# Key sums of an attention layer turned round on TensorE, with GpSimd adds for the token sums and new plan constants

## The chip, the core and the metric

One core of one Trainium2 chip runs the whole program in one launch. The metric is the device time in microseconds. Three runs of the kernel before took 996.18, 996.35 and 997.45 us; their median, 996.35 us, is the time before.

## What is computed

Random-feature attention feeds a two-layer network with a softplus between the layers (8 batches, 8 heads, 576 tokens, 64 per head, 128 features; 4608 tokens in all, widths 512 and 2048):

```python
def phi(x):
    h = np.einsum('bhsd,md->bhsm', x, omega) - np.sum(x * x, axis=-1, keepdims=True) / 2.0
    return np.exp(h - np.max(h, axis=-1, keepdims=True)) / np.sqrt(m)
q_p, k_p = (phi(q_s), phi(k_s))
kv = np.einsum('bhsm,bhsd->bhmd', k_p, v)
z = np.sum(k_p, axis=2)
num = np.einsum('bhsm,bhmd->bhsd', q_p, kv)
den = np.einsum('bhsm,bhm->bhs', q_p, z)[..., None] + 1e-06
x = (num / den)                       # tokens x 512
h = x @ w_in
y = (np.maximum(h, 0.0) + np.log1p(np.exp(-np.abs(h)))) @ w_out
```

The two sums of the keys are what the change touches: `kv` (features by head width, one matrix for each head) and `z` (the sum of the key features over the tokens).

## The kernel before, in words

Four heads of one batch are a "quad" (`Quad`), so each batch has two and the program has sixteen. The tokens of a quad come in five units: units 0 to 3 hold 128 tokens of each of the four heads, unit 4 the last 64. A unit of keys is loaded, projected onto the features (lines 445 and 588), exponentiated into a tile `ph`, and then summed: `plan_keys` collects the units and `plan_sums` plans their products, units 0 to 2 in one go and units 3 and 4 in a second. In `outer` (line 676) the features of 128 tokens are the stationary operand, 128 columns wide, and the values of the same tokens with a column of ones, 65 columns, are streamed. So one product gives `kv` with features on partitions, and `z` as its last column. Every fp32 product that is no transpose stands twice in a trace; one unit of four products is eight rows of line 676. `part` (682) copies the first go out on ScalarE; `z` (686), `z_turn` (690) and `whole` (694) add the second go on VectorE; `out_z` and `in_z` (700, 704) send `z` through memory to spread it over all partitions.

The queries go the same way up to `ph`, are divided by their denominator (`den` 784, `divide` 794), turned in blocks through memory, and multiplied by `kv` in `plan_both` (954), `plan_x` (997) and `plan_late_x` (1048). There the stationary operand is 64 columns wide and the two heads of a pair write the lower and the upper half of the output partitions. The first batch has a way of its own (735, 868, 877, 922).

The network's two layers are products of 512 columns in three parts each (high by high, high by low, low by high; lines 1412 to 1414 and 1441 to 1443, and 1199 and 1256 to 1258 for the last pair of token blocks). They are most of TensorE's work. `ident` and `idle` products (line 1571, "fill") compute nothing that is used; they stand where the planner expected TensorE to wait in the first 228 us.

The order of every engine is fixed while the program is built. Each piece of work is a `do(...)` with a cost, a due time and what it comes after; `in_order` takes the works one by one, by the engine that could start first and among its candidates by due time, and gives out buffers by name (`room`). The due times are a table (`KEYS`, `QUERIES`, `IN`, `OUT`) plus a constant at each `do`. GpSimd and VectorE share a port to memory, so works marked `port` are put in order with each other.

## Time and profile before

| | us |
|---|---|
| median of three runs | 996.35 |
| profiled execution, first to last instruction (span) | 995.2 |
| TensorE busy | 989.6 |
| VectorE busy | 783.6 |
| ScalarE busy | 722.7 |
| GpSimd busy | 206.4 |

The page gives no other time of the profiled execution than its span; the median of the runs is 1.15 us above it. TensorE's rows overlap: a product of 512 columns is shown as 0.39 us long, while the next one starts 0.227 us later. So what a product costs is read from start to start, not from its length. A group's cost below is the time from the start of the last wide product before it to the start of the second wide product after it, less two steps of 0.227 us: the first wide product after a group is often followed late, and that belongs to the group.

### The profile page before, as it was taken

To read this page: it belongs to the slowest core of one execution; us is meant where nothing else is said; L and a number is where in the kernel's file an instruction comes from. 1 tells how busy PE (TensorE), PEld (TensorE's weight loads), DVE (VectorE), ACT (ScalarE), POOL (GpSimd) and SP (SyncE) were. 2 spreads that over 40 slices of the span, in tenths; PEclk is the share of its full clock that TensorE was granted. 3 is DMA by queue.
4 is the path that set the end of the run, shared out by engine and by line. 5 is a ranking of instruction groups with operands and counts; after the bars stand their busy time and mean duration, and the time that the engine had idled before them with its cause. 6 is when DMAs were issued, how large, how long until landed. Compare 5 with 4: busy or idle time off the path is not lost.

```text
span 995.2 us, 17488 instructions
## 1 busy us (share of the span) xinstructions
PE 989.6 (99%) x5495; PEld 830.9 (83%) x5495; DVE 783.6 (79%) x2306; ACT 722.7 (73%) x1794; POOL 206.4 (21%) x235
## 2 busy tenths in 40 slices
PE   9999999999999999999999999999999999999998
PEld 8988888888888888888878888888888878888886
DVE  6899986889898888888879886887787958676620
ACT  7999887879777777877777776776776656666520
POOL 3313232312221122101212121112011214223000
PEclk9999999999999999999999999999999999999999
DMA  9982355454464455543454444434542331000011
GB/s 321 352 282 90 111 162 152 138 160 141 136 183 139 125 138 160 159 128 113 138 144 133 123 129 119 155 106 113 138 141 75 80 92 43 0 1 1 1 43 42
DMA packets 117628, 124.49 MB, mean 125 GB/s; under 512 B 16288, under 2 KB 93728, under 8 KB 117536
## 3 DMA queue, kind: packets, MB, share of 16 engines
q1 hardware_dynamic: 117392, 123.26, 41.4%
q8 instruction: 43, 0.70, 0.3%
q14 instruction: 49, 0.40, 0.1%
q10 hardware_dynamic: 144, 0.13, 0.0%
HBM read 97.37 MB, written 25.98 MB: 124 GB/s over the span
## 4 chain that ended last, share of the span: by engine, by line
PE 98%; DVE 1%; ACT 0%; issue 0%
PE banks L1441 11%; PE banks L1412 11%; PE banks L1442 10%; PE banks L1443 10%; PE banks L1413 10%; PE banks L1414 10%; PE banks L1199 8%; PE banks L676 5%; PE banks L588 5%; PE banks L1256 3%; PE banks L1258 3%; PE banks L1257 3%; PE banks L445 2%; PE banks L997 2%; PE banks L735 1%; PE banks L954 1%
## 5 line engine op out<-in xcount | busy, mean ns | idle before, releaser
L1412 PE MATMUL banks<-xh,wi 128*128 128x512 f32 (+1 forms) x512 | 188.8, 369 | 0.4 <-DVE u L1427 0.4
L1413 PE MATMUL banks<-xl,wi 128*128 128x512 f32 (+1 forms) x512 | 186.1, 363 | 0.0
L1414 PE MATMUL banks<-xh,wi 128*128 128x512 f32 (+1 forms) x512 | 185.9, 363 | 0.0
L1441 PE MATMUL banks<-wo,gh 128*128 128x512 f32 x448 | 178.6, 399 | 0.0
L1442 PE MATMUL banks<-wo,gh 128*128 128x512 f32 x448 | 175.5, 392 | 0.0
L1443 PE MATMUL banks<-wo,gl 128*128 128x512 f32 x448 | 175.0, 391 | 0.0
L1418 ACT ACTIVATE u<-banks 128x512 f32<-128x512 f32 (+1 forms) x128 | 70.1, 548 | 73.4 <-PE banks L1414 60.5
L1412 PEld LDWEIGHTS banks<-xh,wi 128*128 128x128 f32 x512 | 96.4, 188 | 17.2 <-issue 1.2
L1414 PEld LDWEIGHTS banks<-xh,wi 128*128 128x128 f32 x512 | 96.4, 188 | 15.6
L1413 PEld LDWEIGHTS banks<-xl,wi 128*128 128x128 f32 x512 | 96.6, 189 | 13.9
L1441 PEld LDWEIGHTS banks<-wo,gh 128*128 128x128 f32 x448 | 84.2, 188 | 18.5 <-issue 4.3
L1443 PEld LDWEIGHTS banks<-wo,gl 128*128 128x128 f32 x448 | 84.1, 188 | 18.5
L1442 PEld LDWEIGHTS banks<-wo,gh 128*128 128x128 f32 x448 | 84.4, 188 | 13.3
L1427 DVE SCALAR_TENSOR_TENSOR u<-banks,u 128x512 f32<-128x512 f32 (+1 forms) x128 | 78.4, 613 | 15.8 <-ACT u L1424 15.4
L612 ACT ACTIVATE phq<-phq,smq 128x128 f32<-128x128 f32 x216 | 71.8, 395 | 14.7 <-DVE smq L608 14.7
L794 POOL TENSOR_TENSOR phq<-phq,dnq 128x512 f32<-128x512 f32 (+1 forms) x46 | 41.9, 911 | 189.2 <-DVE dnq L790 113.1
L612 ACT ACTIVATE phk<-phk,smk 128x128 f32<-128x128 f32 x216 | 71.9, 397 | 10.7 <-DVE smk L608 10.7
L784 DVE CUSTOM_DVE_ANT_0 restq<-phq,zb 128x128 f32<-128x128 f32 x280 | 72.7, 293 | 4.8 <-ACT phq L612 4.0
L1421 ACT ACTIVATE u<-u 128x512 f32<-128x512 f32 (+1 forms) x128 | 74.4, 581 | 1.8
L1424 ACT ACTIVATE u<-u 128x512 f32<-128x512 f32 (+1 forms) x128 | 74.6, 584 | 1.3
L1431 ACT CAST gh<-u 128x512 fp32r<-128x512 f32 (+1 forms) x97 | 55.8, 576 | 18.0 <-PE banks L1442 17.1
L1435 POOL TENSOR_TENSOR gl<-u,gh 128x512 fp32r<-128x512 f32 (+1 forms) x41 | 45.1, 1101 | 106.4 <-ACT gh L1431 31.5
(224 smaller groups left out, 2097.3 us busy)
## 6 DMA issues: line engine op xcount, KB each, us to landing
xk<-ky SPq DMA_DIRECT2D x48, 384.0 KB
xq<-qy SPq DMA_DIRECT2D x48, 384.0 KB
qdq<-restq SPq DMA_DIRECT2D x56, 256.0 KB
out<-o SPq DMA_DIRECT2D x36, 256.0 KB
vk<-vv SPq DMA_DIRECT2D x70, 130.0 KB
rawi<-wi SPq DMA_DIRECT2D x16, 512.0 KB
rawo<-wo SPq DMA_DIRECT2D x16, 512.0 KB
q<-qdq SPq DMA_DIRECT2D x64, 128.0 KB
```

Of the source, the lines that this page charges most:

```text
L612: nc.scalar.activation(b["ph"][:, c], b["ph"][:, c], AF.Exp, bias=b["sm"][:, 2, c : c + 1])
L784: i = nc.vector.tensor_tensor_reduce(jk[r, c], ph[r, c], q.zb[r, h], 1.0, 1e-6, ALU.mult, ALU.add, dn[r, 0, c : c + 1])
L1199: nc.tensor.matmul(b[key], x, y, start=fresh and not kk and not n, stop=kk == 1 and n == 2, skip_group_check=True)
L1412: nc.tensor.matmul(b["h"], wh, xh[:, cc, t], start=cc == 0, stop=False)
L1413: nc.tensor.matmul(b["h"], wh, xl[:, cc, t], start=False, stop=False)
L1414: nc.tensor.matmul(b["h"], wl, xh[:, cc, t], start=False, stop=cc == NCC - 1)
L1421: nc.scalar.activation(b["u"], b["u"], AF.Exp, scale=-1.0)
L1424: nc.scalar.activation(b["u"], b["u"], AF.Ln, bias=1.0)
L1427: nc.vector.scalar_tensor_tensor(b["u"], b["h"], 0.0, b["u"], ALU.max, ALU.add)
L1441: nc.tensor.matmul(acc[tt], gh, w2[fc][:, 0], start=fc == 0, stop=False)
L1442: nc.tensor.matmul(acc[tt], gh, w2[fc][:, 1], start=False, stop=False)
L1443: nc.tensor.matmul(acc[tt], gl, w2[fc][:, 0], start=False, stop=fc == NFC - 1)
```

## The change

In `plan_sums` the operands change places: 64 columns of values are the stationary operand, the 128 features are streamed, and the two heads of a pair write the two halves of the output partitions. `kv` then stands with the head width on partitions and has to be transposed (`kv_turn`, two transposes a quad) and copied (`kv_turned`). The column of ones is gone. `z` is made in two ways. In the second batch (two quads) TensorE makes it with a 32 column stationary operand of ones, four products a unit, into the same bank. In the six batches after it GpSimd adds the feature tiles of the five units (`plan_z`, four adds with the last one in two halves), and `kv_turn` sums that tile over the partitions with four products of 32 columns. `z_row` copies the result, and `out_z` sends it in one transfer instead of four.

Beside that: query blocks of over 256 columns are loaded in two pieces (before, over 320); tiles are laid out so that nearly all large ones start at 448 modulo 512 bytes, where `xh` and `xl` stood at 192 and others at 0, 64, 128, 256 and 320; weight loads may come right behind the first key load; and nearly every cost and due time of the planner has another number, so that the order of all engines is another.

```diff
-KEYS = ((-130.35, -33.11, -44.26, -126.91, -51.00), (-184.12, -170.41, -56.38, -80.88, -261.61))
+KEYS = ((-681.34, -192.75, -318.79, -174.84, -200.15), (-576.11, -262.69, -529.96, -206.80, -300.25))
...
+        if apart:
+            for x in loads:
+                x.behind = ld
...
+        def add():
+            add_ = nc.gpsimd.tensor_tensor
+            x = b["ph", i]
+            if u == 1:
+                q.z = at.tile([P, 4, M], F32, name=f"z{q.nm}", tag=q.z_slots["z"], bufs=1)
+                b0, i0, _ = q.z_first
+                return add_(q.z, b0["ph", i0], x, ALU.add)
+            if u < 4:
+                return add_(q.z, q.z, x, ALU.add)
+            for j in (1, 0):
+                r, h = slice(j * D, (j + 1) * D), slice(2 * j, 2 * j + 2)
+                a_ = add_(q.z[r, h], q.z[r, h], x[r, :2], ALU.add)
+            return a_
...
-            for c in range(4 if u < 4 else 2):
-                end = k == len(keys) - 1 and c == (3 if u < 4 else 1)
-                cs = slice(c, c + 1) if u < 4 else slice(c, 4, 2)
-                nc.tensor.matmul(kv[:, cs], ph[:, c], v[:, cs], start=not k and not c, stop=end, skip_group_check=True)
+            end = k == len(keys) - 1
+            for p in range(2):
+                for j in range(2):
+                    r, c = (slice(0, P), 2 * j + p) if u < 4 else (slice(j * D, (j + 1) * D), p)
+                    nc.tensor.matmul(
+                        kv[j * D : (j + 1) * D, p], v[r, c], ph[r, c], start=not k and not p, stop=end, skip_group_check=True
+                    )
+            for c in range(4 if na > 2 else 0):
+                nc.tensor.matmul(
+                    kv[32 * c : 32 * (c + 1), 2], (ones if u < 4 else halves[:, c // 2 : c // 2 + 1]).broadcast_to([P, 32]),
+                    ph[:, c if u < 4 else c % 2], start=False, stop=end, skip_group_check=True,
+                )
...
+        def kv_turn():
+            y["turned"] = y["bank"][:, 2 * M if na < 3 else 0 :][:, : 2 * M].rearrange("p (a m) -> p a m", m=P)
+            for p in range(2):
+                nc.tensor.transpose(y["turned"][:, p], q.kvp[:, p], ident)
+            for c in range(0 if na > 2 else 4):
+                nc.tensor.matmul(
+                    y["bank"][32 * c : 32 * (c + 1), :M], ones.broadcast_to([P, 32]), q.z[:, c], start=True, stop=True,
+                    skip_group_check=True,
+                )
...
-            sizes = [w] if w <= 320 else [256, w - 256]
-            kinds = ["q" if w <= 256 else "q1"] if w <= 320 else ["q0", "q1"]
+            sizes = [w] if w <= 256 else [256, w - 256]
+            kinds = ["q"] if w <= 256 else ["q0", "q1"]
```

Where the order of the instructions moves, three places matter.

TensorE at the second go of one quad in the middle of the program (batch 3, first quad): before, units 3 and 4 and what follows (`phk` are key features, `vk` values, `wi`, `xh` and `xl` the first layer's operands).

```order
L676 MATMUL banks<-vk_0_3_3287,phk_0_3_3402 128x65 x4
L676 MATMUL banks<-vk_0_4_3374,phk_0_4_3486 128x2x65 x2
L1412 MATMUL banks<-xh,wi_1119 128x512
L1413 MATMUL banks<-xl,wi_1119 128x512
L1414 MATMUL banks<-xh,wi_1119 128x512
```

And now, in the same place:

```order
L727 MATMUL banks<-phk_0_3_3444,vk_0_3_3290 64x128 x4
L727 MATMUL banks<-phk_0_4_3545,vk_0_4_3411 64x128 x4
L1489 MATMUL banks<-xh,wi_510 128x512
L1490 MATMUL banks<-xl,wi_510 128x512
L1491 MATMUL banks<-xh,wi_510 128x512
L1489 MATMUL banks<-xh,wi_510 128x512
L1490 MATMUL banks<-xl,wi_510 128x512
L1491 MATMUL banks<-xh,wi_510 128x512
L748 MATMUL banks<-ident,kvp_0_3436 128x128 x2
L750 MATMUL banks<-z_0_3276,small 32x128 x4
```

The go has eight products instead of six, and six wide products after it stands a new group, the two transposes and the four sums of `z`; between the two VectorE runs `whole`.

SyncE's queue of loads at the start, before (`wi` and `wo` are weights, `k` keys):

```order
L241 DMA omf_76<-om 128x128
L324 DMA rawi_115<-wi 128x1024
L413 DMA xk_0_1_117<-k 128x2x260
L505 DMA x_first<-k 128x260
L413 DMA xk_0_2_121<-k 128x2x260
```

And now:

```order
L247 DMA omf_76<-om 128x128
L331 DMA rawo_120<-wo 128x1024
L331 DMA rawo_122<-wo 128x1024
L331 DMA rawi_124<-wi 128x1024
L517 DMA x_first<-k 128x260
L421 DMA xk_0_1_145<-k 128x2x260
L421 DMA xk_0_2_147<-k 128x2x260
```

Three weight loads of 512 KB, not one, stand ahead of the second key unit.

TensorE in the same stretch, before, from the first fill to the second quad's second key unit:

```order
L1571 MATMUL banks<-ident 128x512
L445 MATMUL banks<-omf,xk_0_1_117 128x128 x4
L457 MATMUL banks<-small,xk_0_1_117 128x56 x4
L1571 MATMUL banks<-ident 128x512
L445 MATMUL banks<-omf,xk_0_2_121 128x128 x4
...
L1571 MATMUL banks<-ident 128x512 x2
L445 MATMUL banks<-omf,xk_1_0_127 128x128 x4
L457 MATMUL banks<-small,xk_1_0_127 128x56 x4
L1571 MATMUL banks<-ident 128x512 x3
L445 MATMUL banks<-omf,xk_1_1_140 128x128 x4
```

And now:

```order
L1648 MATMUL banks<-ident 128x512 x10
L454 MATMUL banks<-omf,xk_0_1_145 128x128 x4
L466 MATMUL banks<-small,xk_0_1_145 128x56 x4
L1648 MATMUL banks<-ident 128x512
L454 MATMUL banks<-omf,xk_0_2_147 128x128 x4
...
L1648 MATMUL banks<-ident 128x512 x8
L454 MATMUL banks<-omf,xk_1_0_153 128x128 x4
L466 MATMUL banks<-small,xk_1_0_153 128x56 x4
L454 MATMUL banks<-omf,xk_1_1_155 128x128 x4
```

The fills on `ident` are 27 in all now, and were 9; the ten on `idle` ahead of everything are the same.

## Rows read from the trace of the kernel before

**Rows 1.** The page: its head, and busy time of each engine.
```profile
span 995.2 us, 17488 instructions
PE 989.6 (99%) x5495; PEld 830.9 (83%) x5495; DVE 783.6 (79%) x2306; ACT 722.7 (73%) x1794; POOL 206.4 (21%) x235
```
**Rows 2.** The chain that ended last: shares of the span by engine.
```profile
PE 98%; DVE 1%; ACT 0%; issue 0%
```
**Rows 3.** Windows: stretch, length, PE, PEld, DVE, ACT, POOL, clock, DMA share, GB/s.
```profile
6.00:20.00 14.00, 13.94 (x169) 11.95 (x168) 8.99 (x30) 11.39 (x40) 5.62 (x9) 1.00 1.04 356
400.00:500.00 100.00, 100.00 (x511) 84.26 (x510) 86.14 (x270) 77.84 (x196) 17.51 (x22) 1.00 0.47 136
```
**Rows 4.** Timeline, TensorE: first and last of 24 wide products; start, length, instruction.
```profile
420.53 0.39 PE L1441 MATMUL banks<-wo,gh 128*128 128x512 f32 x1
...
425.74 0.39 PE L1414 MATMUL banks<-xh,wi 128*128 128x512 f32 x1
```
**Rows 5.** Timeline, TensorE: first go of a quad's key sums, units 0 to 2.
```profile
196.30 0.39 PE L1414 MATMUL banks<-xh,wi 128*128 128x512 f32 x1
196.53 2.79 PE L676 MATMUL banks<-vk,phk 128*128 128x65 f32 x24
...
199.44 0.39 PE L1442 MATMUL banks<-wo,gh 128*128 128x512 f32 x1
```
**Rows 6.** Timeline, TensorE: second go, units 3 and 4.
```profile
212.76 0.40 PE L1443 MATMUL banks<-wo,gl 128*128 128x512 f32 x1
212.99 1.50 PE L676 MATMUL banks<-vk,phk 128*128 128x65 f32 x12
...
214.56 0.40 PE L1442 MATMUL banks<-wo,gh 128*128 128x512 f32 x1
```
**Rows 7.** Timeline, TensorE: eight narrow products (64 columns stationary) over 128 columns.
```profile
668.90 0.39 PE L1443 MATMUL banks<-wo,gl 128*128 128x512 f32 x1
669.22 1.09 PE L954 MATMUL banks<-q,kvs 128*64 128x128 f32 x16
...
670.58 0.40 PE L1442 MATMUL banks<-wo,gh 128*128 128x512 f32 x1
```
**Rows 8.** The same, over 256 columns.
```profile
383.85 0.39 PE L1414 MATMUL banks<-xh,wi 128*128 128x512 f32 x1
384.17 1.95 PE L954 MATMUL banks<-q,kvs 128*64 128x256 f32 x16
...
386.39 0.40 PE L1442 MATMUL banks<-wo,gh 128*128 128x512 f32 x1
```
**Rows 9.** Timeline, TensorE: four transposes, and what starts after them.
```profile
25.52 0.60 PE L868 MATMUL banks<-ident,xq 128*128 128x128 f32 x4
25.95 1.04 PE L735 MATMUL banks<-xk 128*128 128x256 f32 x4
```
**Rows 10.** Groups by form: fills on `ident`; busy, mean ns, idle before.
```profile
L1571 PE MATMUL banks<-ident 128*128 128x512 f32 x9 | 3.7, 462 | 0.1
```
**Rows 11.** Timeline, TensorE: three fills, and the product behind them.
```profile
13.10 0.96 PE L1571 MATMUL banks<-ident 128*128 128x512 f32 x3
13.99 0.71 PE L445 MATMUL banks<-omf,xk 64*128 64x128 f32 x8
```
**Rows 12.** Timeline, TensorE: a wait early in the first layer, and its releaser.
```profile
60.34 0.39 PE L1412 MATMUL banks<-xh,wi 128*128 128x256 f32 x1 [0.40 <-DVE u L1427]
```
**Rows 13.** Groups by form: late wide products with their moving tile at different places.
```profile
L1199 PE MATMUL banks<-xl,wi 128*128 128x512 f32 x64 | 25.0, 390 | 0.0
L1199 PE MATMUL banks<-b,wi 128*128 128x512 f32 x48 | 12.4, 393 | 0.0
```
**Rows 14.** Groups by form: GpSimd add, full and half; `whole` on VectorE.
```profile
L1435 POOL TENSOR_TENSOR gl<-u,gh 128x512 fp32r<-128x512 f32 x27 | 34.9, 1291 | 66.4 <-ACT gh L1431 17.9 <-DVE gh L1431 10.7 <-PE banks L588 9.7
L582 POOL TENSOR_TENSOR tq<-xq,tq 64x256 fp32r<-64x256 f32 x8 | 5.9, 738 | 20.7 <-ACT tq L578 14.5 <-DVE tq L578 6.0
L694 DVE SCALAR_TENSOR_TENSOR kvs<-banks,kvp 128x256 f32<-128x256 f32 x14 | 5.8, 413 | 0.0
```

More of the change, by code (lines that the diff above doesn't have):

```diff
@@ L254, in favor_softplus_kernel @@
     make_identity(nc, eye)
+    for i in range(4):
+        at.tile([P, 3, 8], F32, name=f"sm{i}", tag=f"sm.{i}", bufs=1)
+    at.tile([P, 16], F32, name="gap1")
     nc.gpsimd.tensor_copy(dense, eye)
@@ L260, in favor_softplus_kernel @@
     halves, ones = small[:, :2], small[:, 2:3]
+    for i in range(4):
+        const.tile([P, 4, 4], F32, name=f"dn{i}", tag=f"dn.{i}", bufs=1)
     xh = const.tile([P, NCC, RING], F32R, name="xh")
@@ L357, in plan_weights @@
         l = do(
-            "SP", dma(0.65, 1.60, 1.7), due + 87.17, load, spare={} if last else {"w": 2},
+            "SP", dma(0.65, 1.28, 1.7), due + 110.47, load, spare={} if last else {"w": 2},
             take=[({"i": "qh", "o": "ql"}[nm] if last else "w", box, "raw")],
         )
+        loads.append(l)
         if last:
@@ L614, in plan_split @@
         ld = do(
-            "SP", read(n * (P + D) * P * 4), due - 89.77, load, behind=prev.get("load"), take=[("x", b, "x")],
+            "SP", read(n * (P + D) * P * 4), due - 417.96, load, behind=prev.get("load"), take=[("x", b, "x")],
         )
@@ L661, in plan_keys, with plan_z @@
                 q.keys, q.key_deps = [], []
+    def plan_z(q, b, i, u, due, es):
+        if q.b < 2:
+            return
+        b["uses", ("phs", i)] = 2
+        if not u:
+            q.z_first, q.z_slots = (b, i, es), {}
+            return
+        def add():
[11 more added lines that the diff above has]
+            return a_
+        give = [(b, ("phs", i))]
+        if u == 1:
+            b0, i0, es0 = q.z_first
+            give.append((b0, ("phs", i0)))
+            after = es + es0
+        else:
+            after = es + [q.z_last]
+        q.z_last = do(
+            "POOL", pool(512) if u < 4 else 2 * pool(256), due - 163.51, add, after=after, give=give,
+            take=[("z", q.z_slots, "z")] if u == 1 else [],
+        )
     def plan_sums(q, keys, due, deps):
@@ L698, in out_z @@
-            for i in range(4):
-                r = slice(i * 32, (i + 1) * 32)
-                nc.sync.dma_start(q.zd[:, r], q.zr[i * 32 : i * 32 + 4])
+            q.zd = dram.tile([4, M], F32, name=f"zd{q.nm}", tag="zd", bufs=2)
+            nc.sync.dma_start(q.zd, q.z[::32, 0] if na < 3 else q.kvp[::32, 2])
         def in_z():
@@ L711, in plan_sums @@
             m = do(
-                "PE", 0.86 if u < 4 else 0.43, due - 235.34, lambda k=k: outer(k), after=[m] if k else [x for x, _ in deps],
-                soon={} if k else dict(deps), take=[] if k else [("at" if q.b > 1 else "more", y, "bank")],
+                "PE", (0.50 if u < 4 else 0.31) + 0.30 * (na - 2) + (0 if k else 0.10), due - 259.72, lambda k=k: outer(k), after=[m] if k else [x for x, _ in deps],
+                soon={} if k else dict(deps), take=[] if k else [("at" if q.b > 1 else "more", y, "at")],
                 give=[(b, ("phs", i)), (b, ("vs", i))], heat=1040,
@@ L933, in plan_early_x @@
         t = do(
-            "PE", 0.45 if tail else 0.46, due - 227.12, turn, after=[d for _, d in rows], heat=1024, behind=prev.get("turn_x"),
+            "PE", 0.45 if tail else 0.46, due - 389.27, turn, after=[d for _, d in rows], heat=1024, behind=prev.get("turn_x"),
             take=[("any", y, "b")], give=[(b, "x") for b, _ in rows],
@@ L1349, in plan_pair @@
-            q2 = do(*dp(2 * P), sdue - 139.44, lambda e, b=b: sums(e, 2, b), after=[q1, f1], port=True)
-            q3 = do(*dp(2 * P), sdue - 44.26, lambda e, b=b: sums(e, 3, b), after=[q2], give=[(b, ("tag", "f2"))], port=True)
-            q4 = do(*dp(2 * P), sdue - 32.45, lambda e, b=b: sums(e, 4, b), after=[q2], port=True)
+            sdue = due - 280.32
+            f1 = do(*dp(TB), sdue + 436.12, lambda e, b=b, j=j, nm=nm: whole(e, b, "f1", j, nm), after=gate + [done_w["i", j]], take=[("two", b, ("tag", "f1"))], port=True, behind=pe.get((5, j - 2)))
@@ new lines, in plan_pair @@
+            f2 = do(*dp(TB), sdue + 524.21, lambda e, b=b, j=j, nm=nm: whole(e, b, "f2", j + H, nm), after=gate + [done_w["i", j + H]], take=[("two", b, ("tag", "f2"))], port=True, behind=f1)
+            q1 = do(*dp(2 * P), sdue + 48.46, lambda e, b=b, nm=nm: sum1(e, b, nm), after=[f2], take=[("two", b, ("tag", "R"))], port=True)
+            q2 = do(*dp(2 * P), sdue + 363.85, lambda e, b=b: sums(e, 2, b), after=[q1, f1], port=True)
+            q3 = do(*dp(2 * P), sdue - 20.48, lambda e, b=b: sums(e, 3, b), after=[q2], give=[(b, ("tag", "f2"))], port=True)
```

327 lines of the change are left out of this document (171 added, 156 removed).

## The prediction, made before the changed kernel ran

> **What bounds the kernel now.** I read the page's head first: TensorE is busy 99% of a span of 995.2 us, the next engine 79% [rows 1]. The chain of waits agrees, with 98% of it on TensorE [rows 2]. The windows tell that this holds from early on: TensorE is busy 13.94 of 14.00 us even between 6 and 20 us, and all of 400 to 500 us, at a granted clock of 1.00, which is the 2.4 GHz level [rows 3]. So nothing that another engine gains is worth anything here, and anything that TensorE gains or loses, at the start or later, moves the end by as much. The sum below therefore counts TensorE's time alone. Of the other engines it asks only whether TensorE comes to wait for them.
>
> The unit is the wide product of 512 columns: 24 of them start 5.21 us apart from first to last, 0.227 us each [rows 4].
>
> **The key sums, twelve quads.** Before, a first go costs 199.44 - 196.30 - 2 x 0.227 = 2.69 us [rows 5] and a second one 1.35 us [rows 6], 4.04 us a quad. The new shapes do not stand in the trace; the nearest are narrow groups, 64 columns stationary, where two products write the two halves of the output partitions. Eight of them cost 1.23 us over 128 columns [rows 7] and 2.09 us over 256 [rows 8]. The difference over 8 x 128 more columns gives 0.1075 us per product over 128 columns, and the rest, 0.37 us, is the change of shape into the group and out of it, or 0.185 us a change.
>
> - First go, 12 such products: 12 x 0.1075 + 0.37 = 1.66 us.
> - Second go, four such products and four that have only 64 rows. If these four cost as much as the others it is 1.23 us; if half, 1.02 us; with one more change of shape between them, 1.42 us. I take 1.12 us, the middle of the first two.
> - The turn: two transposes at 0.11 us (four start 25.95 - 25.52 = 0.43 us apart from what follows [rows 9]), a change in and out, and four sums of `z`, 32 columns wide. If four of those run side by side, as the pairs of 64 do [rows 7], they cost 0.215 us; if only two, 0.43 us. So 0.80 to 1.02 us; I take 0.86 us, near the lower end, since the pairs show that products on different output partitions overlap.
>
> Together 3.64 us (3.48 to 4.10) for 4.04 us: -0.40 us a quad, -4.8 us for twelve (-6.7 to +0.7).
>
> **The two quads of the second batch.** They have 20 more products, 32 wide, at 0.054 to 0.1075 us (1.08 to 2.15 us), and eight changes between 64 and 32 wide inside the goes; the turn has its transposes alone. Without price for the changes it is 1.66 + 1.02 + 1.08 + 0.22 = 3.98 us; with both shapes at their dear end and 0.185 us a change it is 1.66 + 1.42 + 2.15 + 0.22 + 1.48 = 6.93 us. I take 1.66 + 1.12 + 1.08 + 0.22 and half a change, 0.09 us, eight times: 4.8 us, so +0.8 us a quad, +1.6 us for both (-0.1 to +5.8).
>
> What speaks against the whole edit is that it changes the shape of TensorE's tile far more often, and each change of shape that the trace shows has cost 0.185 us. The Trainium skill says so too, in "TensorEngine Tiling (Array Packing)", section "Tiling Modes": a change of the tiling mode drains TensorE, while a change of tile within a mode does not. By it the dear ends above hold; the trace bears it out at a group's ends [rows 7], and no row shows a change between 32 and 64.
>
> **The start.** Three weight loads of 512 KB (128 x 1024 numbers of four bytes) stand now ahead of the second key unit, where one stood. The queues already move 356 GB/s between 6 and 20 us [rows 3], so 1.05 MB more is 2.9 us later for the keys. The program stands in for this with 18 more fills. At the steady step of 0.227 us these are 4.1 us; nine fills of before are 3.7 us busy, 0.41 us each [rows 10], which would make 7.4 us; three in a row took 13.99 - 13.10 us, 0.30 us each, to the next product [rows 11]. Fills only help the sum where something useful comes earlier for it, and I see nothing but one wait of 0.40 us on VectorE in the first layer [rows 12] that may go. I take +3.5 us, between the bytes and the steady step (2.9 to 7.4), and -0.4 us for that wait.
>
> **Small terms on TensorE.** Two more projection groups of 64 rows, each with a change in and out: 2 x 0.37 = +0.7 us. One query block in two pieces instead of one: +0.3 us, one change more and a little. Tile places: the late products whose moving tile stood elsewhere are 393 ns long against 390 ns [rows 13]; with some 180 products placed so, 3.3 ns each, that is -0.6 us (0 to -2, where the places cost nothing or three times this).
>
> **What costs nothing while its cover holds.** GpSimd's adds are 36 full ones at 1.29 us and 24 halves at 0.74 us [rows 14], 64 us on an engine that works 206 of 995 us [rows 1]. They hold the feature tiles longer, until the last add; if that were late, the next exponentials would wait and then the projections. VectorE loses `z` and `z_turn` and gets the copy `kv_turned` or leaves it to ScalarE: even. SyncE sends one `z` transfer instead of four, and loads no column of ones; its queue is only full at the start. The new wait is on TensorE: `kv_turn` needs `whole` (0.413 us [rows 14]), which needs the second go. Between them stand mostly six wide products, 1.36 us, and everything behind `kv_turn` on TensorE is queued behind that wait. VectorE's mean operation is 86.14 / 270 = 0.32 us [rows 3], so `whole` is in time with two operations ahead of it and late with three.
>
> **Sum.** -4.8 + 1.6 + 3.5 - 0.4 + 0.7 + 0.3 - 0.6 = +0.3 us on the span of 995.2 us, so 995.5 us. The median of the runs is 1.15 us above that span; carried along, 996.35 + 0.3 = **996.7 us**: no change, where 0.2%, 2.0 us, is about what a measurement of this kernel can tell.
>
> **Rivals.**
>
> Faster: the new shapes overlap fully (halves at half price, four `z` sums at once, changes inside a group free), the second batch comes out at -0.2 us, and the start costs only its bytes. Then -6.7 - 0.2 + 2.9 + 0.0 = -4.0 us, where the small terms cancel: 992.3 us. For it stand the pairs of 64 [rows 7], against it that no four were seen at once. Chance 0.37.
>
> Slower, at the start: fills and late keys at the full 7.4 us, everything else as summed: +4.2 us, 1000.6 us. It decides for slower once the start costs over 5.2 us. For it: the fills of before were 0.41 us each, and DMA is at its limit there; against it: fills in a row took 0.30 us. Chance 0.15.
>
> Slower, by changes of shape: each one inside a group drains the array, and halves and `z` sums go at the dear ends. The outer part is then +0.7 + 5.8 = +6.5 us and the sum +10.0 us, 1006.4 us. It decides once the twelve quads save nothing. This is the rule named above. Chance 0.08.
>
> Slower, by the new wait: with five operations ahead of `whole` TensorE waits 0.413 + 5 x 0.32 - 1.36 = 0.65 us at each of 14 turns, 9 us, 1005.7 us. It decides from the fourth one on (0.33 us a quad, 4.7 us). Against it: such a queue would have to stand there in most quads, and VectorE has idle time. Chance 0.05.
>
> That the edit does not do what it says is excluded by the order of TensorE's instructions: every quad has the new groups.
>
> **How the numbers follow.** The forecast, no change within 2.0 us, has 0.35. Faster has 0.37, slower 0.15 + 0.08 + 0.05 = 0.28. The range reaches below the first rival by its unknown tile places, to 990.5 us, and above the second to 1002 us; it leaves out the two dear rivals and a little on the lower side, 0.17. The forecast's own range is 994.4 to 998.4 us.
>
> **What would show it.** A first go at 1.66 us, a second at 1.0 to 1.2 us, a turn at 0.8 to 0.9 us, and the second batch's quads at 4 to 5 us, measured from wide product to wide product as above, would bear out the terms; a turn with idle time before it, ended by VectorE, would bear out the last rival. The first wide products of the network should begin some 3 to 4 us later than now. Wrong it would be if the steady step of 0.227 us changed, since most of TensorE's time hangs on it: 1% of the span is 10 us. Wrong too if the work beside TensorE, moved by the new due times, let it wait anywhere after the first 100 us.

## The result, and the profile after

The changed kernel takes 1003.90 us (median of four runs, 1003.79 to 1004.47) against 996.66 us of the kernel before beside it: a ratio of 1.0073, with a 95% interval of 1.0061 to 1.0085. That is 7.2 us slower, 1.9 us above the upper end of the forecast range. The profiled execution has a span of 1002.0 us, 6.8 us more than before.

The page's head and its line of engines, which answer to [rows 1]:

```profile
span 1002.0 us, 18215 instructions
PE 993.7 (99%) x5805; PEld 814.5 (81%) x5805; DVE 798.3 (80%) x2305; ACT 715.9 (71%) x1790; POOL 286.1 (29%) x296
```

The windows, which answer to [rows 3] (stretch, length, TensorE, its weight loads, VectorE, ScalarE, GpSimd, granted clock, DMA share, GB/s):

```profile
6.00:20.00 14.00, 11.40 (x114) 9.00 (x112) 9.34 (x24) 10.59 (x31) 4.39 (x8) 1.00 1.06 362
400.00:500.00 100.00, 100.00 (x556) 81.04 (x556) 87.32 (x274) 77.20 (x199) 36.27 (x37) 1.00 0.50 140
```

TensorE is still busy all of 400 to 500 us, and GpSimd's 80 us of new work cost it nothing there. Between 6 and 20 us it is busy 11.40 us where it was 13.94, with 20 of the 27 fills on `ident` among its work, where seven of nine were. Two lists give all that TensorE waited for (us in total, times, longest), first in the kernel before, then in the changed one, where three of the four lines lie in the first 17 us:

```profile
PE banks L1571 <- DVE small L263: 1.1, 1, 1.1
PE banks L1412 <- DVE u L1427: 0.4, 1, 0.4
PE banks L877 <- DVE xl L931: 0.3, 1, 0.3
```

```profile
PE banks L1648 <- ACT xk L504: 1.6, 1, 1.6
PE banks L1648 <- DVE small L274: 1.1, 1, 1.1
PE banks L454 <- DMA xk<-k: 1.0, 1, 1.0
PE banks L995 <- DVE xq L968: 0.5, 1, 0.5
```

The waits grow from 1.8 to 4.2 us in all. Where did 6.8 us come from? I took every step of TensorE from one product's start to the next one's start, in both traces, and summed them by the lines of this table. Where a wide product is followed by one of another line, it counts 0.227 us and the rest of the step goes to the other line; a wait behind a narrow product stays with that product. The first wait, 1.05 us in both, is left out.

| TensorE, us | before | after | |
|---|---|---|---|
| fills, the ten on `idle` too | 6.5 | 10.5 | +4.0 |
| projections of the first two batches, with the waits at them | 31.3 | 34.0 | +2.7 |
| the rest of the first batch | 25.6 | 25.8 | +0.2 |
| key sums and turns, batches 1 to 7 | 54.1 | 51.3 | -2.8 |
| first layer, with late first products behind groups | 312.9 | 315.9 | +3.0 |
| projections of the later batches | 51.2 | 51.9 | +0.7 |
| second layer and the last pair, to the end | 479.8 | 478.8 | -1.1 |
| late queries' products | 32.8 | 32.9 | +0.2 |

The first three lines, +6.9 us, are the start: 18 more fills at about the steady step of 0.227 us, 4.1 us, and in the second line the waits of 0.99 and 1.55 us that stand below. Most of the first layer's +3.0 us belongs to narrow groups: the first wide product behind one of the new groups is followed by the next after 0.34 us instead of 0.227, and there are more groups. With it the sums and turns come out at about nothing.

### The profile page after: what moved, and what is told of

It reads as the page before. It is cut to its first block, busy times and chain, and to the rows that moved or that the text cites. A ratio compares the mean times of both kernels' runs of the same rounds, so it can differ in the third digit from the quotient of the medians.

```text
span 1002.0 us, 18215 instructions
## 1 busy us (share of the span) xinstructions
PE 993.7 (99%) x5805; PEld 814.5 (81%) x5805; DVE 798.3 (80%) x2305; ACT 715.9 (71%) x1790; POOL 286.1 (29%) x296
## 4 chain that ended last, share of the span: by engine, by line
PE 96%; DMA 2%; DVE 1%; SPq 0%; issue 0%; ACT 0%; DVEq 0%; ACTq 0%
PE banks L1489 11%; PE banks L1518 11%; PE banks L1490 10%; PE banks L1491 10%; PE banks L1519 10%; PE banks L1520 10%; PE banks L1276 8%; PE banks L600 5%; PE banks L727 4%; PE banks L1333 3%; PE banks L1335 3%; PE banks L1334 3%; PE banks L1074 2%; PE banks L454 2%; PE banks L810 1%; PE banks L1031 1%
## 5 line engine op out<-in xcount | busy, mean ns | idle before, releaser
L1512 DVE TENSOR_TENSOR gl<-u,gh 128x512 fp32r<-128x512 f32 (+1 forms) x105 | 69.0, 658 | 16.0 <-ACT gh L1508 14.5
L594 POOL TENSOR_TENSOR tq<-xq,tq 64x512 fp32r<-64x512 f32 (+1 forms) x45 | 52.1, 1158 | 93.8 <-ACT tq L590 27.7
```

## The experiments

All the versions below are built on the changed kernel, but for one. Where the order was mended by hand, works were moved in the finished list of works, so that every engine's order but for the moved ones stays as it was.

### The start: early weights and fills

Two loads moved behind the key loads with their work, fills left out, and both:

```diff
+        if nm == "o" and fc in (1, 7):
+            moved[0].append(l)
+            moved[1].extend([a, b, c, d, lp])
...
+    order = [w for w in order if w not in moved[0] and w not in moved[1]]
+    for ws, at_ in zip(group, (raws[1][1], raws[1][2])):
+        i = order.index(at_)
+        order[i:i] = ws
...
         if isinstance(w, tuple):
-            w[0](*w[1:])
             continue
```

Here `raws[1]` is the load of the next weight and its first step of work; the last line taken away is the fills' call.

> The changed kernel with two of its three leading weight blocks (the loads and their work on ScalarE, VectorE and GpSimd) put behind the key loads, and all else in the same order, the 27 fills on ident too. Theory (the start costs some 6 us, part by late keys, part by the fills that were planned for late keys): the keys come 2 to 3 us earlier, but the fills still stand in front of their products, so 1.0 to 3.0 us less than 1003.9, 1001 to 1003. Rival (only the late keys cost): 4 to 6 us less, 998 to 1000. Second rival (the cost lies in the key sums, the start is made up for later): within 0.7 us of 1003.9.

> The changed kernel without its 27 fills on ident, all else in the same order; they compute nothing that is used. Theory (late keys and fills together): TensorE waits for the late keys where the first ten fills stood, and only the later fills are saved: 1.5 to 4 us less than 1003.9, 1000 to 1002.4. Rival (the fills only fill waits): within 0.7 us. Second rival (the fills keep TensorE's clock up): a granted clock below 1.00 before 60 us and a longer time than 1003.9.

> Both edits, the two weight blocks behind the key loads and no fills on ident. Theory: both parts of the start's cost go, 5 to 7 us less than 1003.9, 997 to 999. Rival (only fills cost): the same as without fills alone, within 0.7 us. Rival (the start is made up for later): within 1 us of 1003.9.

Measured: 1008.15 us with the late weights (ratio to before 1.0114, 1.0099 to 1.0129), 1007.36 without fills (1.0107, 1.0092 to 1.0122), 1005.46 with both (1.0088, 1.0072 to 1.0105). All three are slower than the changed kernel. No theory had that; of the rivals one had, the second of the version without fills, with a clock under 1.00 and a longer time. With late weights the clock stays at 1.00 in the profiled run. The keys land early, but their products still start at 9.74 us, behind the ten fills, and the second quad's at 17.84 us where it was 18.20. By the sums above 2.6 us of the loss of 3.9 us in the span lie in the first batch's sums and queries: TensorE waits there 1.63 us for exponentials, which ScalarE does only behind a weight's work that now stands at 20.8 to 24.1 us. What the other two tell is in the timelines of TensorE (start, length, instruction, idle time before it and what ended that): the second key unit and the second quad's first products, without fills, and then without fills and with late weights.

```profile
9.03 0.71 PE L454 MATMUL banks<-omf,xk 64*128 64x128 f32 x8 [1.99 <-DMA xk<-k]
...
17.15 1.52 PE L454 MATMUL banks<-omf,xk 64*128 64x128 f32 x7 [1.43 <-ACT xk L504]
```

```profile
6.00 0.71 PE L460 MATMUL banks<-omf,xk 64*128 64x128 f32 x8
...
12.64 1.52 PE L460 MATMUL banks<-omf,xk 64*128 64x128 f32 x7 [2.21 <-ACT xk L510]
```

So the two weight blocks hold the keys back by 3.0 us (9.03 - 6.00), as expected (2.9 us in the sum). But with early keys TensorE waits 2.21 us for exponentials, and in both kernels products that take 0.71 us take 1.52 us afterwards: the clock has fallen. The windows of the first 20 us, without fills and with both edits, have it at 0.74 and 0.78, where the changed kernel has 1.00:

```profile
0.00:20.00 20.00, 14.93 (x106) 13.00 (x108) 10.99 (x34) 11.98 (x31) 5.96 (x15) 0.74 0.97 327
0.00:20.00 20.00, 16.60 (x137) 14.75 (x138) 10.37 (x36) 12.50 (x34) 5.92 (x15) 0.78 0.96 329
```

The fills of the changed kernel do hold the clock in its profiled run; that they cost time of their own doesn't mean that it is saved without them.

The other way round, one part of the change alone in the kernel before: the next two weight loads put ahead of the first.

```diff
+    r = [w for w in order if any(w is x for x in raws)]
+    order = [w for w in order if w not in r[1:3]]
+    i = order.index(r[0])
+    order[i:i] = r[1:3]
```

> The kernel before with one part of the change alone: the next two weight loads put ahead of the first one and so ahead of the second key unit, three loads of 512 KB as in the changed kernel; the order of everything else is that of before. Theory (three early loads hold the keys back and are the first cause of the long start): the second key unit's products start about 3 us later than 7.46 us, and the time grows by 2.5 to 4 us with TensorE's clock at 1.00, by 5 to 9 us if the wait also lets the clock fall; 999 to 1006. Rival (the start's cost is in the plan of the other engines, the bytes alone are absorbed): within 1.5 us of before.

Measured: 1008.30 us, ratio 1.0111 (1.0098 to 1.0124), 11.4 us more than before and over the upper end of 999 to 1006. The timeline of TensorE and the window behind it:

```profile
8.73 1.23 PE L446 MATMUL banks<-omf,xk 64*128 64x128 f32 x8 [1.76 <-DMA xk<-k]
```

```profile
10.00:20.00 10.00, 10.00 (x70) 8.26 (x68) 4.61 (x17) 5.68 (x21) 5.57 (x9) 0.50 1.05 331
```

The keys' products are 1.3 us later than the 7.46 us of before, less than the 3 us expected. The keys themselves are 2.3 us later (ScalarE's squaring of them starts at 8.71 us where it was 6.38); in the kernel before they lay ready for a while. The idle time of 1.76 us ahead of them puts the clock at 0.50, the 1.2 GHz level, for all of 10 to 20 us, and it is still 0.50 in 20 to 25 us. Fifteen microseconds at half clock are up to 7.5 us of work, in a profiled run whose span is 9.1 us over that of before. The bytes are the smaller part of the price here, and the clock is the larger one; the changed kernel's profiled run, at 1.00, doesn't pay this price.

### The edge of the clock, and the key sums

```diff
-                    r, c = (slice(0, P), 2 * j + p) if u < 4 else (slice(j * D, (j + 1) * D), p)
+                    c = 2 * j + p
...
-        "vv": np.concatenate(_rows(v[1:]), axis=3),
+        "vv": _rows_apart(v[1:]),
```

> The changed kernel with the last unit's four products on all 128 rows: the values of the other head's 64 tokens come as zeros from memory, four columns loaded instead of two; same sums, same order, no 64x64 tile any more. Theory (a change from 128x64 to 64x64 tiles inside the second go costs about 0.15 to 0.2 us): the second go falls from 1.38 to 1.23 us in twelve quads and by 0.2 to 0.4 us in the two of the second batch, so 1.8 to 2.8 us less, 1001.1 to 1002.1. Rival (products with 64 rows cost half, and the change nothing): the go grows to 1.5 us or more, 1004 to 1006.

```diff
-            for c in range(4 if na > 2 else 0):
+            for b_, i_, u_ in keys if end and na > 2 else []:
+                for c in range(4):
```

> The changed kernel with the 32 column products for the token sums of the second batch put behind all other products of their go instead of behind each unit's; all else in the same order. Theory (each change between 64 and 32 columns costs about 0.15 us): eight changes a quad become three, so 1.3 to 2.0 us less for the two quads, read from start to start in the trace; by the total 1002 to 1002.6 if the clock stays at 1.00 in the first 30 us. Rival (a change inside a group is free): nothing.

> The changed kernel itself, unaltered, beside the others on the same chip. Both theories: 1003.5 to 1004.5; a run some us longer, with a granted clock under 1.00 in the first 30 us, would show that its start is on the edge of losing the clock, as in the kernels with grouped token sums (1002.5 to 1009.5) and with 128 row products.

The totals were 1006.99 us (1004.67 to 1007.32) with the 128 row products, 1003.54 (1002.51 to 1009.54) with the grouped token sums and 1004.52 (1003.67 to 1009.48) for the changed kernel itself: too wide for what they were to tell. The spread is the clock. The changed kernel's run of 1009.48 us had a granted clock of 0.993 over its span, that of 1003.67 one of 0.999; 0.006 of 1002 us is 6.0 us, and the two differ by 5.8. In the profiled run with 128 row products TensorE stood idle 1.35 us ahead of the late keys, 0.36 us longer than the 0.99 us of the changed kernel, and 10 to 15 us went at 0.74, 15 to 20 at 0.50. With grouped token sums there is next to no wait for the keys (fills up to 9.5 us, products from 9.62), and the clock falls all the same, behind the wait of 1.55 us for a bank that the changed kernel has at the same place without a fall. The eight fills behind it take 3.41 us, where they take 2.14 us in the changed kernel (below), and 15 to 20 us go at 0.66:

```profile
15.97 3.41 PE L1650 MATMUL banks<-ident 128*128 128x512 f32 x8 [1.55 <-ACT xk L504]
```

So the changed kernel's start lies on an edge: waits of about the same length let the clock fall in one execution and not in another, and that decides over several microseconds.

The groups themselves are free of that. The second go of a quad, in the changed kernel and with 128 row products, TensorE's timeline:

```profile
421.37 0.40 PE L1491 MATMUL banks<-xh,wi 128*128 128x512 f32 x1
421.70 1.24 PE L727 MATMUL banks<-phk,vk 128*64 128x128 f32 x16
422.87 0.50 PE L1518 MATMUL banks<-wo,gh 128*128 128x512 f32 x1
423.21 0.40 PE L1519 MATMUL banks<-wo,gh 128*128 128x512 f32 x1
```

```profile
425.17 0.40 PE L1490 MATMUL banks<-xh,wi 128*128 128x512 f32 x1
425.50 1.09 PE L726 MATMUL banks<-phk,vk 128*64 128x128 f32 x16
426.52 0.50 PE L1517 MATMUL banks<-wo,gh 128*128 128x512 f32 x1
426.86 0.39 PE L1518 MATMUL banks<-wo,gh 128*128 128x512 f32 x1
```

From the last wide product to the second one after the group, less two steps of 0.227 us, that is 1.38 us and 1.23 us, also as means of three quads with nothing beside the go. Four products with 64 rows cost what four with 128 rows cost, and the change from 128x64 to 64x64 tiles 0.15 us more. The second batch bears the first out: there each unit's four products follow a change of shape anyway, and they take 0.58 us to the next group's start with 128 rows (77.79 to 78.37 us) as with 64 (78.73 to 79.31).

A first go of the second batch in the changed kernel, and with the token sums grouped:

```profile
68.91 0.39 PE L1520 MATMUL banks<-wo,gl 128*128 128x512 f32 x1
69.22 0.66 PE L727 MATMUL banks<-phk,vk 128*64 128x128 f32 x8
69.81 0.43 PE L731 MATMUL banks<-phk,small 128*32 128x128 f32 x8
70.17 0.66 PE L727 MATMUL banks<-phk,vk 128*64 128x128 f32 x8
70.75 0.42 PE L731 MATMUL banks<-phk,small 128*32 128x128 f32 x8
71.11 0.66 PE L727 MATMUL banks<-phk,vk 128*64 128x128 f32 x8
71.70 0.43 PE L731 MATMUL banks<-phk,small 128*32 128x128 f32 x8
72.05 0.39 PE L1489 MATMUL banks<-xh,wi 128*128 128x256 f32 x1
```

```profile
70.29 0.39 PE L1522 MATMUL banks<-wo,gl 128*128 128x512 f32 x1
70.61 1.53 PE L727 MATMUL banks<-phk,vk 128*64 128x128 f32 x24
72.07 0.86 PE L733 MATMUL banks<-phk,small 128*32 128x128 f32 x24
72.86 0.38 PE L1491 MATMUL banks<-xh,wi 128*128 128x256 f32 x1
```

The same products take 72.05 - 68.91 = 3.14 us with five changes inside the go and 72.86 - 70.29 = 2.57 us with one: 0.14 us a change. Eight more 32 column products add 0.79 - 0.36 = 0.43 us, 0.054 us each, so four of them do run side by side. In the table's terms the grouping took 1.42 us and the 128 rows 1.61 us off the line of the key sums, at the lower end of 1.3 to 2.0 and just under the 1.8 us that were expected. All of the 1.61 us comes from the six batches with GpSimd's sums: in the second batch, where 0.2 to 0.4 us a quad were expected, the 128 rows gain nothing, since the 32 column products stand between the units there and the change of shape stays.

Whether such a gain comes through to the total, a last version was to show, with both edits and 15 fills instead of ten ahead of the late keys:

```diff
+    order = [(*w[:2], 15 if w[2] == 10 else w[2]) if isinstance(w, tuple) else w for w in order]
```

> The changed kernel with the grouped token sums and the 128 row products, and 15 fills instead of ten in front of the second key unit, so that TensorE stands idle for less there. Theory (the idle time there is what lets the clock fall in some runs; the sums' gain is TensorE's own): all runs with a clock of 1.00, and the 3.0 us that the two edits took off their groups show in the total, 1000.5 to 1002. Rival (more fills delay the keys' products as much as they save): 1003 to 1005.

Measured: 1002.85 us, ratio 1.0059 (1.0045 to 1.0072), runs of 1001.02 to 1003.53. The two runs with a clock of 1.00 and 0.999 took 1001.02 and 1001.25 us, 2.7 us under the changed kernel's 1003.8 us at the same clock: the gain comes through. That the fills would hold the clock in all runs, with 1000.5 to 1002 us, fell; in three of five it was 0.998.

### Planned anew

```diff
-OUT = (-96.18, -1261.07, -392.69, -10.91, 173.24, -181.69, 229.77, -1194.93, ...
+OUT = (-96.18, -101.07, -392.69, -10.91, 173.24, -181.69, 229.77, -94.93, ...
```

> The changed kernel with two numbers of its table of due times altered (the second and the eighth of OUT, -1261.07 and -1194.93, become -101.07 and -94.93), and planned anew: one weight load instead of three stands ahead of the second key unit, as in the kernel before, and the planner asks for 34 fills on ident instead of 27. Theory (the three early weight blocks are what delays the start, and the plan made for them its length): keys from 7.5 us on, clock 1.00 throughout, 3 to 6 us less than 1003.9, 998 to 1001. Rival (the first 100 us are bound by ScalarE and VectorE, and weight work that is not done in the first 10 us must be done there): no gain or a loss, 1003 to 1008, as with the two blocks moved by hand.

> The altered due times together with the 128 row products for the last unit and the grouped token sums. Theory: these two take 1.6 to 2.0 us and 1.3 to 2.0 us off the altered due times alone, 995 to 998. Rival (TensorE's gains in the first 100 us are lost again to waits there): 1.5 to 2.0 us off alone, from the quads after 100 us.

Measured: 1022.42 us, ratio 1.0264 (1.0246 to 1.0282), and 1012.93 us, 1.0167 (1.0150 to 1.0184). The start has the order of the kernel before, and it doesn't help: with two numbers of the table changed, all later work stands in another order, and TensorE waits in the middle of the program, where both kernels have no wait at all. The window of the first of the two, to be read beside the one above:

```profile
400.00:500.00 100.00, 97.67 (x526) 78.20 (x525) 82.69 (x256) 73.14 (x187) 31.48 (x32) 0.98 0.49 139
```

So this is no undoing of one part, and it tells nothing on the start's price. The second is 9.5 us under the first, far more than its two edits took off above: its order is another one again. A third version, with the second batch's token sums on GpSimd too, took 1023.96 us, but what it computes is off by 28%, so its time stands for no version of this kernel. What these runs do tell is that two numbers of the plan cannot be changed here without the rest.

### Mending the start by hand

The remaining runs kept the plan and mended the first 25 us: two weights' loads behind the key loads, one fill for ten, five and later two for the eight ahead of the second quad, and the order on ScalarE and VectorE step by step. In the code `key(h, u, i)` is a step of key unit `u` of the first (0) or second (1) quad: its squarings (`sq`), exponentials (`ex`), less-norms and bias steps (`ln`, `bi`) and maxima (`mx`); `chains` are the two weights with their five steps. Each move names works, the one that they are put at, and whether before (0) or behind it (1). The first mending moves only the loads, three squarings and the weights' work; the order unit by unit came with the third version, of which these are the moves:

```diff
+    moves = [([c[0] for c in chains], marks["q", 0, 0][ld], 0)]
+    moves += [([key(0, u, ln), key(0, u, bi)], key(0, u, mx), 1) for u in range(5)]
+    moves += [(key(0, 1, ex), key(0, 0, ex)[1], 1), ([key(1, 0, sq)], key(0, 2, ex)[1], 1)]
+    moves += [([key(1, 2, sq)], key(0, 4, ex)[1], 1), ([key(1, 3, sq)], key(0, 3, ex)[1], 1)]
+    moves += [([w for w in order if any(w in c[1:6] for c in chains)], key(0, 4, ex)[1], 1)]
```

The fourth version changes the place in the last line alone. The last three change it too, and beside that put the second quad's less-norms and bias steps on VectorE unit by unit and two squarings of queries behind the second quad's exponentials; the last two also move a third weight's work. All but the first have the sums' edits.

> The changed kernel with the order of its first 25 us mended by hand: two of the three leading weight loads behind the key loads and their work behind the second quad's first exponentials, three squarings of late keys on ScalarE behind the exponentials that they stood ahead of, ten fills ahead of the second key unit cut to one and eight ahead of the second quad to five. Theory (late keys, then the plan made for late keys): the second quad's products start at 12 instead of 18.2 us, and 3 to 6 us are gained, 998 to 1001. Rival (ScalarE is full from 20 to 100 us, the weight work moved there costs as much): 1002 to 1008.

> The mended start together with the 128 row products of the last unit and the grouped token sums. Theory: 2.5 to 3.5 us less than the mended start alone, 995 to 998. Rival (TensorE's gains are eaten by waits): within 1 us of the mended start.

> A start mended further: as before the two weight loads stand behind the key loads, and now also VectorE's and ScalarE's steps of the first quad follow unit by unit (maximum, norms, bias, exponential), as in the kernel before, the two weights' work behind the first quad's last maxima; two fills ahead of the second quad. With grouped token sums and 128 row products. Theory (the start's cost is late keys and, behind them, exponentials that wait for one another and hold the banks): the second quad's products start at 12 to 13 us with no wait over 1 us, the clock stays at 1.00, 994 to 998. Rival (the weight work on ScalarE has to be done by 100 us and costs the same wherever it stands): 1001 to 1004.

> The same with the two weights' work behind the first quad's last exponentials. Theory: 994 to 999; it tells whether that work in the first quad's exponentials, or behind them, is the dearer place. Rival as for the run ahead of it: 1001 to 1004.

> As the mended start of 1000.4 us, where one squaring of the third key unit of the second quad stood behind the two weights' work on ScalarE and held TensorE for 1.95 us: now the second quad's squarings stand ahead of that work, the second quad's steps on VectorE follow unit by unit too, and two squarings of queries stand behind the second quad's exponentials. The two weights' work stands behind the first quad's exponentials. Theory (in-order queues of ScalarE and VectorE set the start): the waits of 1.95 and 0.98 us go, 995.5 to 998.5. Rival (the weights' work costs the same wherever it stands): 999 to 1002.

> The same with the work of three weights (those two and the next) behind the exponentials of the second quad's third unit. Theory: no wait over 0.6 us before 20 us, 995 to 998; a wait moved to the second quad's last two units would show as 1 to 3 us between 20 and 28 us. Rival: 999 to 1002.

> The same with the next weight's work behind the exponentials of the second quad's fourth unit. Theory: 994.5 to 997.5, at or under the kernel before. Rival: 999 to 1002.

| version | us (runs) | ratio to before | longest wait of TensorE in 11 to 31 us |
|---|---|---|---|
| first mending | 1006.35 (1005.45 to 1006.97) | 1.0098 (1.0083 to 1.0112) | 1.55 |
| the same, with the sums' edits | 1004.23 (1002.60 to 1004.53) | 1.0071 (1.0058 to 1.0084) | 1.55 |
| unit by unit, work behind the first quad's unit 4 | 1000.39 (1000.21 to 1001.83) | 1.0039 (1.0025 to 1.0053) | 1.95 |
| the same, work behind the first quad's unit 3 | 1005.55 (1003.92 to 1007.33) | 1.0088 (1.0073 to 1.0103) | 3.29 |
| the second quad unit by unit too, queries' squarings later, work behind the squaring of the second quad's unit 3 | 1000.96 (999.40 to 1005.37) | 1.0043 (1.0031 to 1.0055) | 2.27 |
| the same, work of three weights behind the second quad's unit 1 | 1003.02 (1002.47 to 1003.38) | 1.0062 (1.0044 to 1.0080) | 3.06 |
| the same, the third weight's work behind unit 3 | 1003.71 (1003.15 to 1003.81) | 1.0066 (1.0050 to 1.0082) | 3.39 |

The first mending brought the second quad's products from 18.20 to 16.13 us, not to 12: ScalarE stood idle 2.44 us for VectorE, whose bias steps were planned behind the maxima of later units, and TensorE's next bank hung on those exponentials. The sums' edits took 2.1 us off it, where 2.5 to 3.5 were expected. In order unit by unit they came at 12.42 us, and that version was the fastest with the sums' edits in, 3.8 us under the first mending with them. The last four say why it went no further. TensorE's timelines in the fourth, the sixth and the seventh version (the fifth has its wait of 2.27 us at 19.95 us):

```profile
19.34 0.80 PE L1654 MATMUL banks<-ident 128*128 128x512 f32 x1 [3.29 <-ACT xk L506]
```

```profile
27.75 1.24 PE L456 MATMUL banks<-omf,xq 64*128 64x128 f32 x7 [3.06 <-ACT xk L506]
```

```profile
30.53 1.41 PE L949 MATMUL banks<-ident,xq 128*128 128x128 f32 x4 [3.39 <-ACT xq L506]
```

ScalarE's timelines say what it does ahead of them. In the fourth version it stands idle itself, for a load of queries whose squarings stand ahead of the exponentials; in the fifth for VectorE's step on the same weight, in the middle of the weights' work:

```profile
17.47 0.79 ACT L437 ACTIVATE xq<-xq 128x256 f32<-128x256 f32 x2 [3.72 <-DMA xq<-q]
```

```profile
19.01 0.62 ACT L358 CAST wo<-rawo 128x512 fp32r<-128x512 f32 x1 [2.53 <-DVE rawo L352]
```

In the sixth and the seventh the exponentials stand behind weights' work as well. So in four of the five versions in order unit by unit the weights' work holds up what TensorE needs next, at 17.7 to 30.5 us, and in one a query's load does; moving the work moves the wait and doesn't shorten it. In all of these profiled runs the granted clock falls behind the wait. The "rival" of these expectations, that the weight work costs the same wherever it is put, isn't borne out by the totals: only the fifth version lies in the range given for it, and the five medians go from 1000.39 to 1005.55 us, with the clock. The theory's 994 to 998 us was not reached by any median, and no version beat the kernel before. The fifth came nearest in single runs: 999.40, 999.95 and 1000.03 us, at a clock of 1.00. That is only 1.0 to 1.6 us under the 1001.02 us that the version with 15 fills took at that clock, with the same sums and its start not mended. So at full clock this mending gives back little of the start's 6.9 us.

## Why the prediction was wrong

The forecast was 996.7 us, a change of +0.3 us, as the sum of a gain of 3.2 us in the key sums and a loss at the start. Both terms were mis-sized, both to the slow side: the sums gave about nothing, and the start took 6.9 us instead of 3.5. Each measured value lies inside the ends given for its term. The range held one term at its dear end and not both.

**The bound.** That TensorE sets the end was right, also in the changed kernel. That "nothing that another engine gains is worth anything here" failed at the start: there ScalarE's and VectorE's queues decide when banks come free. The windows of before showed TensorE busy there; they could not show that it was so because the other engines' order suited it.

**Twelve quads.** The first go was forecast at 1.66 us and measured 1.67 (mean of eleven), the turn 0.86 and 0.78. So the step from narrow groups was sound, and four 32 column products do run side by side. The second go failed: 1.12 us was taken, the middle between half price and full price for products with 64 rows, and it is 1.38 us. There is no half price, and the change of tile inside the go is paid. The quad comes to 3.83 us instead of 3.64, which saves 0.215 us and not 0.40: -2.6 us instead of -4.8.

**The second batch.** A quad takes 5.3 us (3.03 for the first go, 2.28 with the turn), not 4.8, so +2.5 us for both and not +1.6. I took half a change, 0.09 us, inside the goes; it is 0.14 to 0.15 us. This was the rule weighed against the change, that a change of mode drains TensorE, in the Trainium skill, "TensorEngine Tiling (Array Packing)", section "Tiling Modes". The runs agree with it in that a change costs time: 0.14 and 0.15 us inside a group, against 0.185 us at a group's ends in the trace of before. Its rival at 1006.4 us took all dear ends at once; the halves and the changes were near theirs, the 32 column products were not.

**The start** is the step that failed most. The bytes were priced rightly, 2.9 us for the keys, and 3.0 us is what two weight blocks do to them. The fills were too, 4.1 us at the steady step, and 4.0 us is what they take. But 3.5 us was taken as a price for the whole, "between the bytes and the steady step" of the fills, as if the fills stood in for the late keys and no wait came beside them. The waits of 0.99 and 1.55 us, 2.5 us together, were put at nothing; the first is what the ten fills don't cover of the late keys, and the second, for ScalarE, is in neither price. In the changed kernel's TensorE they follow one another:

```profile
6.22 2.57 PE L1648 MATMUL banks<-ident 128*128 128x512 f32 x10
9.78 0.71 PE L454 MATMUL banks<-omf,xk 64*128 64x128 f32 x8 [0.99 <-DMA xk<-k]
...
16.13 2.14 PE L1648 MATMUL banks<-ident 128*128 128x512 f32 x8 [1.55 <-ACT xk L504]
18.20 0.72 PE L454 MATMUL banks<-omf,xk 64*128 64x128 f32 x8
```

Before, these products started at 7.46 and 11.95 us:

```profile
7.46 0.72 PE L445 MATMUL banks<-omf,xk 64*128 64x128 f32 x8
...
11.95 0.71 PE L445 MATMUL banks<-omf,xk 64*128 64x128 f32 x8
```

The lag grows from 2.3 to 6.25 us between the two. Ten fills and a wait stand ahead of the late keys; then a wait of 1.55 us for a bank, then eight more fills. The wait has its reason on ScalarE, where the first exponentials stand behind weight work and the next behind squarings of keys that come late:

```profile
11.68 0.62 ACT L357 CAST wi<-rawi 128x512 fp32r<-128x512 f32 x1
12.21 1.14 ACT L504 ACTIVATE x_first<-banks,smk 128x128 f32<-128x128 f32 x4
13.22 0.43 ACT L435 ACTIVATE xk<-xk 128x256 f32<-128x256 f32 x1
14.28 0.42 ACT L435 ACTIVATE xk<-xk 128x256 f32<-128x256 f32 x1 [0.63 <-DMA xk<-k]
15.02 0.42 ACT L435 ACTIVATE xk<-xk 128x256 f32<-128x256 f32 x1 [0.32 <-DMA xk<-k]
15.45 1.66 ACT L504 ACTIVATE xk<-banks,smk 128x128 f32<-128x128 f32 x6
```

Of the order of these two queues the prediction said nothing; it counted a moved load's bytes and not the work that comes with it on ScalarE and VectorE. The network's first products start at 57.90 us where it was 53.33, 4.6 us later, and not some 3 to 4 us.

**The small terms.** The wait of 0.40 us on VectorE in the first layer [rows 12] went, and one of 0.50 us on another of its steps came. The late products whose tiles moved went from 393 to 390 ns [rows 13]; the last pair's products in the first layer, to which they belong, gained 0.6 us, as forecast, and the rest of that line of the table 0.5 us that was not. The later batches' projections cost 0.7 us, as forecast, and the late queries' products 0.2 us, where 0.3 was forecast for the query block in two pieces. GpSimd's adds and the wait for `whole` cost nothing: no wait stands at any turn in the list of waits above.

**Rivals.** The slow start at 1000.6 us was nearest, with a start of 7.4 us; it kept the sums' forecast gain of 3.2 us, and with nothing there it becomes 1003.8 us. That this is the measured time is luck in part: its 7.4 us were 18 fills at 0.41 us, and what the trace has is fills at the steady step and two waits. The faster rival, at 0.37 the likeliest, needed rows at half price and free changes inside a group, and neither holds.

**What stays open.** The trace tells where the start's 6.9 us lie, 4.0 us in fills and 2.5 in two waits. It doesn't tell what a start without them would take: each version that took fills or early weights away set off the clock or moved the wait, and none gave the time back. That all of it comes from the weights ahead of the keys isn't shown. In the kernel before they cost 11.4 us, but most of that by the clock, as estimated above, and in the changed kernel putting them back made it slower.

## What to carry to other kernels

Price a load that is moved to the front with all that follows it on the other engines' queues, and look for the first place where a busy engine could then fall idle, since what it costs there may be the clock and not the wait. Where two independent terms can each go to their dear end, the range must hold both together. A plan made as a whole may not come apart: here two of its numbers, undone, moved all later work and told nothing about themselves.

## What was not expected of the hardware

TensorE's clock fell after one idle stretch of 1.35 us (128 row products) or 1.76 us (the kernel before with early loads) near 9 to 10 us, and not, in the profiled run, after 0.99 us in the same place. The length alone doesn't tell: a wait of 1.55 us for a bank, near 12 to 16 us, left it at 1.00 in the changed kernel and with late weights, and it went to 0.50 behind the same wait with grouped token sums and in the first mending. It stayed low well after TensorE had work again: 0.50 in 15 to 20 us and 0.73 in 20 to 25 us with 128 row products, 0.50 up to 25 us in the kernel before with early loads. The same program, unaltered, took 1003.67 and 1009.48 us on one chip, at 0.999 and 0.993; which wait let the clock fall in the slower run isn't shown.

Products with 64 rows and 64 columns (1.38 us in a go) cost no less than products with 128 rows and 64 columns (1.23 us, without the change of tile): sending zeros and using all rows is cheaper, where it saves the change.
